# Batch 0 of a fused attention and feed-forward kernel: twelve low planes of the probabilities made by VectorE in place of GpSimd

## The chip, the cores and the metric

The program runs on one core of one Trainium2 chip. A core has TensorE (PE in the profile, PEld for its weight loads), VectorE (DVE), ScalarE (ACT), GpSimd (POOL) and SyncE (SP, which here only issues DMAs). Each engine takes the instructions of its own queue in order, and waits at an instruction until the semaphores of all that it needs are set. The metric is the device time of one execution in microseconds (us).

## The reference

Eight batches, eight heads, 512 local and 32 global positions, head size 64. Local queries see a band of 32 positions to either side and all global keys; global queries see everything. The result goes through a feed-forward layer with the activation h*cos(h).

```python
s_ll = where(|pos_q - pos_k| <= 32, scale * q_l @ k_l.T, -1e9)
s_l  = concat([scale * q_l @ k_g.T, s_ll])        # softmax over both
out_l = softmax(s_l) @ concat([v_g, v_l])
out_g = softmax(scale * q_g @ concat([k_g, k_l]).T) @ concat([v_g, v_l])
x = concat([out_g, out_l])                        # 4352 tokens x 512
h = x @ w_in                                      # 512 -> 2048
out = (h * cos(h)) @ w_out                        # 2048 -> 512
```

All inputs and outputs are float32.

## The kernel before

**Two planes per operand.** A float32 operand of a product is split into a high float16 plane, the rounded value, and a low one, the remainder, and the product is three float16 matmuls (high by high, high by low, low by high). So every operand costs one instruction that writes the high plane and one that writes value minus high.

**Attention.** The heads of a batch go in four pairs, p = 0 to 3, and the 512 queries of a pair in four query tiles, i = 0 to 3. A tile sees a window of 192, 224, 224 or 192 keys. Per pair and tile: `sc_a` computes the scores of both heads (matmul, line 527), `sc_b` adds the mask and takes the row minimum on VectorE (a custom instruction, line 545) into a tile `t` of six rotating buffers, `sc_c` is the exponential on ScalarE with the row sum beside it (line 425), `sc_d` multiplies `t` by the reciprocal row sum (`sm`, lines 564 and 565, on VectorE) and writes the two float16 planes into `planes[i]`, `sc_e` transposes the planes, and `av_a` multiplies them by the values (line 645). In batch 0 the transposition is done on TensorE (line 609), and VectorE (tiles 0 and 2) or ScalarE (tiles 1 and 3) copies the result out of PSUM (line 610). A `t` buffer is free for a later tile as soon as the instruction that computes the low plane has read it.

**Ways to make planes.** `sc_d` takes a code per pair and tile; in batch 0 from the table `PLS`, one row per pair and one entry per tile.

```python
if pl in (3, 4):
    if pl == 3:  # GpSimd scales t, one instruction per head (line 578)
    if pl == 4:  # ScalarE scales t, one instruction per head (line 581)
    nc.scalar.copy(hi, t)                                    # L584, both heads
    for h in range(2):
        nc.gpsimd.tensor_tensor(lo[:, h], t[:, h], hi[:, h], op=ALU.subtract)  # L586
else:
    for h in range(2):
        a = nc.scalar.activation(hi, t[:, h], AF.Identity, scale=r)            # L592
        d = nc.vector.scalar_tensor_tensor(lo, t[:, h], r, hi,
                                           op0=ALU.mult, op1=ALU.subtract)     # L593
```

Pair 3 of batch 0 and all other batches use code 1, the last branch.

**The weights.** `w_in` and `w_out` arrive as float32 in halves or eighths and are split too. For `w_in` the eight pieces k = 0 to 7 are loaded (`w_in_load`, lines 284 and 295), their largest value is taken on VectorE (`w_in_max`, line 246 on `raw_wi`), a scale is derived by a row of very small VectorE instructions (lines 261, 262, 311, 315), and each piece is decoded by ScalarE (line 227) and VectorE (lines 228 and 232) and split by ScalarE (line 239) and GpSimd (line 213). The raw buffers hold four pieces at a time, so a later load waits until GpSimd has read an earlier piece. `w_in_done` turns the largest of all values into the factor `xs` that scales the attention's result (lines 665 and 666), so no product with `w_in` can start before all eight pieces have been looked at. The maxima of `w_out` (line 246 on `wo_hl` and `raw_wm`) are wanted later, for `w_out_done`.

**Order.** From batch 1 on, attention of a later batch is spread between the chunks of the feed-forward part. A chunk is 256 tokens: products `ph` with `w_in` (line 801), activation (lines 823 to 846), products `po` with `w_out` (lines 860 to 862). Ahead of them stands a prologue, in which batch 0's attention and the splitting of `w_in` share VectorE, ScalarE and GpSimd. The code gives each step a slot and a phase, and these become priorities; within them the instructions of each queue are put in order when the program is built, by a planner that keeps a timeline of its own. So a change in one step can also alter the order around it.

Of the kernel before, what the change touches and what calls it, by code (L numbers as in the profile page):

```python
# [62 lines left out]
GFB = 3  # L63
GFW = 3
UW = 1
PLS = [[3, 4, 3, 4], [3, 4, 3, 4], [3, 4, 3, 4], [1, 1, 1, 1]]
TPE = [1, 1, 1, 1]
TPV = [1, 0, 1, 0]
WLV = 0
# [49 lines left out]
def body(tc, qf, v, wi, wo, mask, out):  # L119
# [5 lines left out]
    with ExitStack() as ctx:  # L125
# [441 lines left out]
        def sc_d(b, p, i):  # L567
# [3 lines left out]
            w = WIN[i][1]  # L571
            pl = PLS[p][i] if b == 0 else (PL0, PL1, PL)[min(b, 2)]
            if pl in (3, 4):
# [511 lines left out]
```

## Time and profile before

| | |
|---|---|
| time, median of 3 executions | 959.86 us (959.55 to 961.06) |
| the profiled execution, its own time | 959.23 us |
| its span, first to last instruction | 957.5 us |
| mean granted TensorE clock | 0.965 |
| busy: PE, DVE, ACT, POOL | 909.4, 569.3, 668.4, 399.7 us |

Rows of the profile give the engine, the line of the code, the operation, output and inputs by the program's names, the shapes as partitions x elements, and times. In a timeline row the first number is the start and the second the length, both in us; several instructions of one kind in a row are merged (x4), whatever their shapes, and a bracket says how long the engine had been idle and which instruction released it. In a table of stretches "DVE busy 9.79" is busy time in us within that stretch, and "(x38)" the number of instructions.

### The profile page before, as it was taken

The page shows a single profiled execution, that of the slowest core. Times are in us where ns is not written, and L with a number is a line of the kernel's source. Part 1 is how long each engine was busy: PE and PEld are TensorE (multiplying, and loading weights), DVE is VectorE, ACT ScalarE, POOL GpSimd, SP SyncE. Part 2 cuts the span into 40 slices and gives each one's busy share as a digit, 9 for nine tenths or more (in the row PEclk, how much of TensorE's full clock was granted, in tenths as well). Part 3 has the DMA queues.
Part 4 walks back from the last instruction along what each step waited for, and adds up shares of the span by engine and source line. Part 5 has one row for each costly group of instructions (what it writes and reads, how often), then busy time and mean ns, then how long its engine had stood idle before and what let it go on. Part 6 is the DMA issues. An engine that isn't in the chain of part 4 may idle for free.

```text
span 957.5 us, 20487 instructions
## 1 busy us (share of the span) xinstructions
PE 909.4 (95%) x7963; PEld 604.0 (63%) x7963; DVE 569.3 (59%) x1544; ACT 668.4 (70%) x1435; POOL 399.7 (42%) x412
## 2 busy tenths in 40 slices
PE   6657989999999999999999999999999999999995
PEld 4446656656666666666666666666666666766663
DVE  5987978746565656566655656564746554423231
ACT  7886899957787677766777778777777775443341
POOL 5856654443334243434343333324343434444441
PEclk8667989999999999999999999999999999999998
DMA  9936167745232533545262725342443333000000
GB/s 371 386 121 198 34 163 162 152 111 125 49 108 43 157 63 71 108 122 111 56 122 50 183 46 129 46 146 46 119 61 71 81 68 58 23 1 23 1 24 22
DMA packets 155178, 96.44 MB, mean 101 GB/s; under 512 B 141000, under 2 KB 141128, under 8 KB 153288
## 3 DMA queue, kind: packets, MB, share of 16 engines
q1 hardware_dynamic: 155080, 95.13, 39.6%
q8 instruction: 62, 1.02, 0.4%
q14 instruction: 36, 0.29, 0.1%
HBM read 51.59 MB, written 8.91 MB: 63 GB/s over the span
## 4 chain that ended last, share of the span: by engine, by line
PE 51%; ACT 15%; DVE 11%; issue 9%; POOL 8%; DMA 5%; SPq 0%; ACTq 0%; POOLq 0%; DVEq 0%
PE ph L801 21%; PE po L861 8%; PE po L862 8%; PE po L860 8%; ACT t L425 4%; DMA vr<-v 3%; POOL w L839 3%; PE ps L527 3%; POOL gl L846 2%; ACT planes L592 2%; PE acc L645 2%; DVE gf L841 2%; ACT gh L845 2%; ACT L425 2%; POOL wi_l L213 2%
## 5 line engine op out<-in xcount | busy, mean ns | idle before, releaser
L801 PE MATMUL ph<-xh,wi_h 128*128 128x256 f16 x1024 | 280.7, 274 | 0.9 <-DVE gf L841 0.5
L801 PE MATMUL ph<-xl,wi_h 128*128 128x256 f16 x1024 | 279.8, 273 | 0.0
L801 PE MATMUL ph<-xh,wi_l 128*128 128x256 f16 x1024 | 279.8, 273 | 0.0
L846 POOL TENSOR_TENSOR gl<-gf,gh 128x512 f16<-128x512 f32 x136 | 163.4, 1202 | 237.1 <-ACT gh L845 237.0
L839 POOL TENSOR_TENSOR w<-w 128x512 f32<-128x512 f32 x136 | 143.6, 1056 | 259.1 <-ACT w L425 241.2
L801 PEld LDWEIGHTS <-wi_h 128*128 128x128 f16 x2176 | 205.9, 98 | 55.4 <-issue 18.8
L861 PE MATMUL po<-wo_hl,gh 128*128 128x512 f16 x544 | 206.7, 380 | 0.6 <-POOL wo_hl L213 0.6
L860 PE MATMUL po<-wo_hl,gh 128*128 128x512 f16 x544 | 204.7, 380 | 1.7 <-ACT wo_hl L239 1.7
L862 PE MATMUL po<-wo_hl,gl 128*128 128x512 f16 x544 | 206.3, 380 | 0.0
L845 ACT CAST gh<-gf 128x512 f16<-128x512 f32 x136 | 83.4, 615 | 112.8 <-DVE gf L841 112.7
L824 DVE SCALAR_TENSOR_TENSOR u<-u,cm,ph 128x512 f32<-128x512 f32 x136 | 101.1, 744 | 101.0 <-ACT u L823 101.0
L841 DVE SCALAR_TENSOR_TENSOR gf<-w,ph 128x512 f32<-128x512 f32 x136 | 93.1, 684 | 110.6 <-POOL w L839 110.1
L425 ACT ACTIVATE w<-u,ca 128x512 f32<-128x512 f32 x136 | 98.1, 722 | 84.4 <-DVE u L824 83.5
L425 ACT ACTIVATE t<-t,mn 128x192 f32<-128x192 f32 (+1 forms) x256 | 117.3, 463 | 18.5 <-DVE mn L545 18.1
L801 PEld LDWEIGHTS <-wi_l 128*128 128x128 f16 x1088 | 106.7, 98 | 13.4 <-issue 0.5
L823 ACT ACTIVATE u<-ph,cm 128x512 f32<-128x512 f32 x136 | 92.3, 679 | 25.2 <-PE ph L801 25.2
L593 DVE SCALAR_TENSOR_TENSOR planes<-t,sm,planes 128x192 f16<-128x192 f32 (+1 forms) x232 | 97.8, 481 | 12.0 <-ACT planes L592 11.2
L545 DVE CUSTOM_DVE_ANT_0 t<-ps,msk 128x192 f32<-128x192 f32 (+1 forms) x256 | 83.2, 367 | 18.0 <-PE ps L527 14.8
L862 PEld LDWEIGHTS <-gl 128*128 128x128 f16 x544 | 53.3, 98 | 63.1 <-issue 0.9
L592 ACT ACTIVATE planes<-t,sm 128x192 f16<-128x192 f32 (+1 forms) x232 | 86.3, 458 | 0.0
L861 PEld LDWEIGHTS <-gh 128*128 128x128 f16 x544 | 53.3, 98 | 51.5 <-issue 2.5
L860 PEld LDWEIGHTS <-gh 128*128 128x128 f16 x544 | 52.8, 98 | 51.4 <-issue 2.6
(149 smaller groups left out, 1098.5 us busy)
## 6 DMA issues: line engine op xcount, KB each, us to landing
qkr<-qf SPq DMA_DIRECT2D x31, 608.0 KB, 5.0
vr<-v SPq DMA_DIRECT2D x8, 1280.0 KB, 6.5
out<-o SPq DMA_DIRECT2D x34, 256.0 KB, 2.0
raw_wi<-wi SPq DMA_DIRECT2D x6, 1024.0 KB, 12.2
wo_hl<-wo SPq DMA_DIRECT2D x8, 512.0 KB, 12.7
raw_wm<-wo SPq DMA_DIRECT2D x8, 512.0 KB, 5.7
raw_wo<-wo SPq DMA_DIRECT2D x8, 512.0 KB, 4.4
raw_wi<-wi SPq DMA_DIRECT2D x4, 512.0 KB, 12.3
```

The source lines that it names most:

```text
L425: ins = nc.scalar.activation(*a, **k).ins
L592: a = nc.scalar.activation(hi, t[:, h], AF.Identity, scale=r)
L593: d = nc.vector.scalar_tensor_tensor(lo, t[:, h], r, hi, op0=ALU.mult, op1=ALU.subtract)
L801: nc.tensor.matmul(ph[:, a], w[:, kc, f], x[:, kc, q], start=first and ip == 0, stop=last and ip == 2, skip_group_check=True,)
L824: nc.vector.scalar_tensor_tensor(u, u, m, ph, op0=ALU.subtract, op1=ALU.subtract)
L839: nc.gpsimd.tensor_tensor(w, w, w, op=ALU.mult)
L841: nc.vector.scalar_tensor_tensor(gf, w, 0.5, st.pop(("ph", c, j)).rearrange("p a b -> p (a b)"), op0=ALU.subtract, op1=ALU.mult,)
L845: nc.scalar.copy(gh, gf)
L846: nc.gpsimd.tensor_tensor(gl, gf, gh, op=ALU.subtract)
L860: nc.tensor.matmul(po[k], gh[:, q], wo_h[:, f], start=(f == 0), stop=False)
L861: nc.tensor.matmul(po[k], gh[:, q], wo_l[:, f], start=False, stop=False)
L862: nc.tensor.matmul(po[k], gl[:, q], wo_h[:, f], start=False, stop=(f == NJ - 1))
```

## The change

In the first three pairs of batch 0, tiles 1 and 3 change from code 4 to code 1. Before, ScalarE scaled `t` in place (two instructions), ScalarE copied it into the high plane (one instruction over both heads), and GpSimd subtracted (two instructions). After, ScalarE scales and rounds into the high plane in one step (two instructions), and VectorE multiplies and subtracts in one step (two instructions). Tiles 0 and 2 keep code 3, pair 3 keeps code 1.

```diff
-PLS = [[3, 4, 3, 4], [3, 4, 3, 4], [3, 4, 3, 4], [1, 1, 1, 1]]
+PLS = [[3, 1, 3, 1], [3, 1, 3, 1], [3, 1, 3, 1], [1, 1, 1, 1]]
```

## The prediction

> **What bounds the kernel now.** I read the page first: span, busy times, and the slices.
>
> ```profile
> span 957.5 us, 20487 instructions
> ...
> PE   6657989999999999999999999999999999999995
> ...
> DVE  5987978746565656566655656564746554423231
> ACT  7886899957787677766777778777777775443341
> POOL 5856654443334243434343333324343434444441
> ```
>
> A slice is 23.9 us. From the seventh slice to the last but one TensorE reads 9, so time is won or lost only ahead of that, in the prologue, and there VectorE and ScalarE have the high digits. The changed instructions stand in the first three slices. Next the prologue cut into stretches:
>
> ```profile
> core 0: us, PE busy (x) PEld busy (x) DVE busy (x) ACT busy (x) POOL busy (x), PEclk, DMA share, GB/s
> 24.00:42.00 18.00, 12.78 (x112) 7.80 (x112) 16.54 (x44) 17.02 (x43) 14.17 (x25) 0.54 1.02 414
> 42.00:50.00 8.00, 3.78 (x32) 2.45 (x30) 5.81 (x26) 6.36 (x16) 7.70 (x14) 0.83 1.10 322
> 50.00:54.00 4.00, 1.68 (x14) 1.41 (x14) 3.66 (x7) 4.00 (x10) 2.22 (x2) 0.50 0.95 374
> 54.00:62.30 8.30, 7.42 (x86) 5.66 (x87) 8.20 (x22) 5.88 (x12) 8.23 (x14) 0.58 0.17 70
> 62.30:73.00 10.70, 5.22 (x45) 3.73 (x43) 10.42 (x46) 10.67 (x19) 1.64 (x3) 0.76 0.01 2
> ...
> 84.00:100.00 16.00, 13.51 (x209) 11.03 (x208) 11.69 (x28) 10.55 (x18) 5.69 (x5) 0.89 0.59 195
> 100.00:130.00 30.00, 29.37 (x198) 17.96 (x196) 28.18 (x69) 27.50 (x52) 21.91 (x25) 1.00 0.17 65
> 130.00:200.00 70.00, 65.20 (x556) 40.06 (x555) 55.00 (x165) 68.89 (x164) 28.54 (x32) 0.95 0.69 152
> ```
>
> TensorE is not the bound before 84 us. VectorE is: 8.20 of 8.30 us and then 10.42 of 10.70. ScalarE stands beside it up to 42 us, full up to small gaps. From 100 us TensorE idles only 0.6 and then 4.8 us, so a shift at the end of the prologue reaches the end of the span nearly one to one. Then the timeline, for what makes VectorE idle and who waits for it:
>
> ```profile
> 21.48 0.36 DVE L545 CUSTOM_DVE_ANT_0 t<-ps,msk 128x192 f32<-128x192 f32 x1 [0.21 <-POOL planes L586]
> 32.19 2.40 DVE L232 SCALAR_TENSOR_TENSOR raw_wi<-raw_wi 128x1024 uint32<-128x1024 uint32 x2 [0.79 <-ACT raw_wi L227]
> 37.59 0.39 DVE L545 CUSTOM_DVE_ANT_0 t<-ps,msk 128x224 f32<-128x224 f32 x1 [0.44 <-POOL planes L586]
> 46.62 0.69 DVE L246 TENSOR_REDUCE ws<-raw_wi 128x1 f32<-128x512 f32 x1 [0.42 <-POOL ws L305]
> 49.73 0.39 DVE L545 CUSTOM_DVE_ANT_0 t<-ps,msk 128x224 f32<-128x224 f32 x1 [1.76 <-POOL planes L586]
> 54.10 0.36 DVE L545 CUSTOM_DVE_ANT_0 t<-ps,msk 128x192 f32<-128x192 f32 x1 [0.44 <-POOL planes L586]
> 54.66 1.22 DVE L246 TENSOR_REDUCE ws<-raw_wi 128x1 f32<-128x1024 f32 x1
> 62.33 2.55 ACT L227 ACTIVATE raw_wi<-raw_wi,ws 128x512 f32<-128x512 f32 x3 [2.45 <-DVE ws L262]
> 71.36 12.50 POOL L213 TENSOR_TENSOR wi_l<-raw_wi,wi_h 128x256 f16<-128x256 f32 x16 [9.12 <-ACT wi_h L239]
> ```
>
> The reader is to see two things. Four times VectorE's row minima (L545) wait for a `t` buffer that GpSimd has not yet read, 0.21 + 0.44 + 1.76 + 0.44 = 2.85 us. And from 54.1 us the `w_in` maximum at 54.66 leads, all on VectorE, to the scale for which ScalarE waits 2.45 us (62.33); ScalarE then feeds GpSimd (71.36). So whatever time VectorE has at 54 us is handed on.
>
> **The change part by part.** Durations by shape, between 10 and 80 us:
>
> ```profile
> L586 POOL TENSOR_TENSOR planes<-t,planes 128x192 f16<-128x192 f32 x12 | 8.6, 741 | 5.6 <-ACT planes L584 5.6
> L586 POOL TENSOR_TENSOR planes<-t,planes 128x224 f16<-128x224 f32 x12 | 7.5, 645 | 0.9 <-ACT planes L584 0.9
> L584 ACT CAST planes<-t 128x448 f16<-128x448 f32 x6 | 3.6, 601 | 0.0
> L584 ACT CAST planes<-t 128x384 f16<-128x384 f32 x6 | 3.1, 549 | 0.0
> L581 ACT ACTIVATE t<-t,sm 128x224 f32<-128x224 f32 x6 | 2.6, 504 | 2.7 <-DVE sm L565 2.6
> L581 ACT ACTIVATE t<-t,sm 128x192 f32<-128x192 f32 x6 | 2.5, 474 | 0.0
> L592 ACT ACTIVATE planes<-t,sm 128x224 f16<-128x224 f32 x4 | 1.6, 466 | 0.0
> L592 ACT ACTIVATE planes<-t,sm 128x192 f16<-128x192 f32 x4 | 1.6, 436 | 0.0
> L593 DVE SCALAR_TENSOR_TENSOR planes<-t,sm,planes 128x192 f16<-128x192 f32 x4 | 1.6, 410 | 0.0
> L593 DVE SCALAR_TENSOR_TENSOR planes<-t,sm,planes 128x224 f16<-128x224 f32 x4 | 1.5, 444 | 0.0
> L213 POOL TENSOR_TENSOR wi_l<-raw_wi,wi_h 128x256 f16<-128x256 f32 x26 | 20.1, 805 | 9.1 <-ACT wi_h L239 9.1
> ```
>
> Six tiles change, three of 224 keys and three of 192, two heads each.
>
> GpSimd loses 6 x 0.645 + 6 x 0.741 = 8.3 us. Directly I count this at nothing: GpSimd then idles 9.12 us before 71.36 whatever it did earlier. It counts where somebody waited for it, below. SyncE and GpSimd's queue lose no DMA; a `w_in` load that waits for GpSimd to free a raw buffer may start earlier, but the maximum at 54.66 follows on VectorE without any wait for a DMA, so I count zero; if VectorE came earlier than the data, that load would be the next wait.
>
> ScalarE loses 6 x 0.504 + 6 x 0.474 of scaling and 3 x 0.601 + 3 x 0.549 of rounding, and gains 6 x 0.466 + 6 x 0.436: 9.3 out, 5.4 in, 3.9 us less. After 54 us it waits for VectorE anyway (2.45 us), so this too counts only through VectorE's waits, the 0.79 us at 32.19.
>
> VectorE gains 6 x 0.444 + 6 x 0.410 = 5.1 us, 1.7 us per pair, in the stretches up to 62.30 where pairs 0 to 2 are worked on, on the engine that binds. The rows of these durations lie in a time without GpSimd work (62.30 to 73.00, 1.64 us busy). Behind each low plane stand the next row minima and the weight work in VectorE's queue; its own wait is for ScalarE's high plane. The transposes on TensorE wait for the low plane, and TensorE has room.
>
> What VectorE gets back: of tiles 1 and 3 it now frees the `t` buffer itself, and GpSimd does half the work for the others. I take all four waits, 2.85 us, plus 0.42 at 46.62 (a tiny GpSimd instruction queued behind other GpSimd work) and 0.79 at 32.19: 4.1 us. The lower end is 0 (the waits return, on GpSimd for tiles 0 and 2 or on ScalarE's high plane), the upper end is 4.1, and I take the upper because of what ends the one large wait:
>
> ```profile
> 48.50 1.19 POOL L586 TENSOR_TENSOR planes<-t,planes 128x224 f16<-128x224 f32 x2
> ```
>
> These two end at 49.69, just before VectorE starts at 49.73. Two 224-wide subtractions taken alone, before any 192-wide one of the pair, are those of tile 1, which is a changed tile: its `t` is then free right after VectorE's own low plane.
>
> Last, not all of VectorE's work before 62 us is urgent. The maxima of `w_out` are wanted only after the last one:
>
> ```profile
> 87.99 0.69 DVE L246 TENSOR_REDUCE wos<-raw_wm 128x1 f32<-128x512 f32 x1 [3.47 <-DMA raw_wm<-wo]
> ```
>
> VectorE waits 3.47 us there, and idles 4.31 us between 84 and 100. Each such maximum that slips back there takes its 0.69 us off the urgent stretch. I take one, 0.7 us; ends 0 and two, 1.4.
>
> Sum: 5.1 - 4.1 - 0.7 = +0.3 us. The profiled execution took 959.23 us, which becomes 959.5; the median of the three is 0.63 us above it, so on that footing 960.2 us. This is within 0.2% (1.9 us), which is about what a measurement of this kernel can tell from no change.
>
> **A rule about who blocks whom.** Row first: the 192-wide GpSimd subtraction took 741 ns on the mean, the 224-wide one 645, although it has fewer elements. Some of the 192-wide ones ran beside VectorE's joins of two inputs, until 53.67:
>
> ```profile
> 50.96 2.71 DVE L232 SCALAR_TENSOR_TENSOR raw_wi<-raw_wi 128x1024 uint32<-128x1024 uint32 x2
> ```
>  The Trainium skill, page "SBUF — State Buffer", section "SBUF: two separate sides", says why that can be: GpSimd and VectorE share one pair of ports under an exclusive lock, and a VectorE operation with two SBUF inputs takes part in it, the later one waiting for the whole of the earlier. By that rule the twelve new low planes, each with two inputs, can be held up by GpSimd; the page gives no price for this case. From rows:
>
> ```profile
> L593 DVE SCALAR_TENSOR_TENSOR planes<-t,sm,planes 128x192 f16<-128x192 f32 (+1 forms) x232 | 97.8, 481 | 12.0 <-ACT planes L592 11.2
> ```
>
> Over the whole run, with GpSimd working beside it, the low plane took 481 ns on the mean against 427 for the eight quiet ones: 12 x 0.054 = 0.6 us more. The other end: GpSimd is busy 24.1 of the 30 us from 24 to 54, and half of its 805 ns piece at each meeting makes 12 x 0.8 x 0.4 = 3.9 us. I take neither into the forecast, since twelve GpSimd subtractions that could hold up VectorE go at the same time; it is a rival.
>
> **The rivals.**
>
> *Faster: the chain through GpSimd and ScalarE is what matters.* For it, the chain of waits between 10 and 62 us by line:
>
> ```profile
> by line: POOL planes L586 11.3%; ACT t L425 11.2%; POOL wi_l L213 10.7%; ACT raw_wi L227 8.6%; ACT t L581 8.2%; ACT planes L584 7.6%; ACT vh L476 6.9%; DVE raw_wi L228 5.3%; DVE wos L246 4.6%; DVE pt L610 4.5%; issue 4.5%; DVE ws L246 4.3%;
> ```
>
> Of 52 us L586 has 5.9 and L584 4.0. Half of both goes, 4.9 us. If half of the new low planes, 2.6 us, come onto the chain in their place, 2.3 us are won: 957.6 us. At the most, with all lows hidden, 4.9: 955.0. Against it: VectorE's idle time from 24 to 62.30 is only 4.1 us in all.
>
> *Slower: VectorE's own work.* The low planes stand ahead of the weight work in VectorE's queue and only the waits of the third pair, 1.76 + 0.44, come back, as the others are followed by queues that ScalarE fills: 5.1 - 2.2 = +2.9, 962.8 us. With nothing back, 965.0. It decides against "no change" once less than 3.2 of the 5.1 us come back. For it: after 54.1 us VectorE hardly idles. Against it: the movable `w_out` maxima.
>
> *Slower: the lock.* The 3.9 us above on top of +0.3: 964.1 us. Against it, the measured mean of 481 ns.
>
> *The order changes.* Queues are planned anew, so pieces may change places as far as 200 us; TensorE's idle 4.8 us between 130 and 200 could go or double. This has either sign, I count it in the width of all cases and not as one of its own.
>
> **How the numbers follow.** Forecast, no change to speak of: 0.35. Chain rival: 0.33. VectorE rival: 0.24, lock: 0.08. So faster by over 0.2% 0.33, within 0.35, slower 0.32. The predicted time is 960.2 us. The likeliest case's own range is 958.3 to 961.8. The range over all cases runs from 956.0, which leaves out the last part of the chain rival, to 965.0, VectorE with nothing back; I leave some 2 in 10 outside.
>
> **What would show it.** Right: 24 - 12 = 12 subtractions on GpSimd's L586, 6 on L584, none on L581, 20 low planes on L593 before 80 us at 410 to 480 ns; VectorE's waits for POOL planes down from 2.85 us to under 0.5; the scale for ScalarE at 62.33 within 1 us of where it was, and so the long GpSimd run at 71.36. The chain rival shows both of these earlier by 2 us or more; the VectorE rival later by 2 or more with VectorE busy throughout; the lock in L593 far above 481 ns on the mean before 60 us. What makes the forecast wrong is mostly its second term, the 4.1 us: if the waits turn up again behind ScalarE's high planes, or if removing them lets the whole chain move.

## The result: 0.95% slower, and the profile after

The changed kernel takes 968.29 us (median of 5, 967.79 to 970.5), the kernel before beside it 959.55 us (median of 5). The ratio is 1.0095, 95% interval 1.0079 to 1.011: 9.1 us slower. The forecast was 960.2 us, range 956.0 to 965.0, so the time lies outside it. Below, a difference in us is always (ratio - 1) x 959.6 us.

The head of the page and four of its slice rows, of the changed kernel:

```profile
span 966.0 us, 20485 instructions
...
PE 911.7 (94%) x7963; PEld 607.9 (63%) x7963; DVE 577.7 (60%) x1556; ACT 665.8 (69%) x1429; POOL 393.3 (41%) x400
...
PE   6657988899999999999999999999999999999996
...
DVE  5998978846575666556565656564756555323231
ACT  6895799866777677776777778767777766434341
POOL 4745744423434343433333343424343434344441
```

TensorE reads 9 throughout from the ninth slice on, before from the seventh: slices seven and eight, 145 to 193 us, now read 8. They lie long after the changed steps. The table of stretches of the changed kernel, same stretches as before:

```profile
core 0: us, PE busy (x) PEld busy (x) DVE busy (x) ACT busy (x) POOL busy (x), PEclk, DMA share, GB/s
24.00:42.00 18.00, 12.74 (x100) 8.46 (x97) 16.62 (x48) 17.82 (x39) 12.83 (x21) 1.00 1.09 388
42.00:50.00 8.00, 5.11 (x51) 3.87 (x49) 8.00 (x23) 5.23 (x15) 7.66 (x12) 0.76 0.60 174
50.00:54.00 4.00, 3.05 (x24) 2.42 (x25) 4.00 (x11) 2.33 (x5) 3.44 (x6) 0.50 0.92 349
54.00:62.30 8.30, 6.40 (x69) 5.31 (x68) 8.30 (x24) 8.25 (x22) 0.10 (x1) 0.50 0.73 305
62.30:73.00 10.70, 3.12 (x20) 1.63 (x19) 10.66 (x34) 10.40 (x16) 6.09 (x9) 0.66 0.01 2
84.00:100.00 16.00, 13.23 (x197) 10.88 (x196) 13.14 (x34) 9.41 (x17) 6.16 (x8) 0.82 0.70 217
100.00:130.00 30.00, 29.43 (x204) 18.53 (x203) 26.23 (x59) 24.68 (x51) 21.17 (x24) 0.99 0.19 66
130.00:200.00 70.00, 59.54 (x493) 37.38 (x492) 54.75 (x154) 65.05 (x148) 30.18 (x34) 0.95 0.68 150
```

Two things differ. From 42 to 62.30 us VectorE has no gap left: 8.00, 4.00 and 8.30 us, where it was 5.81, 3.66 and 8.20. And from 130 to 200 us TensorE idles 10.5 us instead of 4.8, while ScalarE, which had idled 2.5 + 1.1 us from 100 to 200, idles 5.3 + 5.0. No instruction there was changed. Two rows of the waits of the changed kernel between 80 and 205 us name the partners (us in total, times, longest):

```profile
ACT w L425 <- DVE u L824: 7.5, 5, 3.4
PE po L860 <- ACT wo_hl L239: 7.0, 5, 2.9
```

and the same two waits of the kernel before:

```profile
ACT w L425 <- DVE u L824: 2.0, 2, 1.2
PE po L860 <- ACT wo_hl L239: 1.7, 2, 1.1
```

ScalarE's longest wait of the first kind, in the timelines of VectorE, GpSimd and ScalarE of the changed kernel:

```profile
111.50 3.57 DVE L512 SCALAR_TENSOR_TENSOR vl<-vr,vs,vh 128x640 f16<-128x640 f32 x2
114.99 0.73 DVE L824 SCALAR_TENSOR_TENSOR u<-u,cm,ph 128x512 f32<-128x512 f32 x1
111.52 2.87 POOL L846 TENSOR_TENSOR gl<-gf,gh 128x512 f16<-128x512 f32 x2
115.76 0.72 ACT L425 ACTIVATE w<-u,ca 128x512 f32<-128x512 f32 x1 [3.40 <-DVE u L824]
```

ScalarE stands still for 3.40 us because the fifth L824 (two of the expectations call it the sixth) stands in VectorE's queue behind four low planes of batch 1's values (L512), the last two stretched to 3.57 us beside GpSimd. In the kernel before, the fifth L824 started at 103.58 us and the sixth at 109.25, both ahead of the first L512 at 110.56. So the planner put the queues in another order here, far from the change. (ScalarE has one longer wait, 6.55 us for VectorE's L410 at 89.74 us; below, a run that wins most of the time back has it too.)

Now the changed planes of the changed kernel, groups between 10 and 80 us:

```profile
L593 DVE SCALAR_TENSOR_TENSOR planes<-t,sm,planes 128x224 f16<-128x224 f32 x10 | 6.3, 676 | 1.5 <-ACT planes L592 1.4
L593 DVE SCALAR_TENSOR_TENSOR planes<-t,sm,planes 128x192 f16<-128x192 f32 x10 | 6.3, 648 | 0.0
L586 POOL TENSOR_TENSOR planes<-t,planes 128x224 f16<-128x224 f32 x6 | 4.9, 833 | 0.0
L586 POOL TENSOR_TENSOR planes<-t,planes 128x192 f16<-128x192 f32 x6 | 4.1, 710 | 1.1 <-ACT planes L584 1.1
```

Counts are as forecast, 20 and 12, but a low plane takes 676 and 648 ns, not 444 and 410. And four rows of its timelines, one from the middle and three from the end of the urgent stretch:

```profile
32.62 1.31 DVE L593 SCALAR_TENSOR_TENSOR planes<-t,sm,planes 128x224 f16<-128x224 f32 x2 [1.38 <-ACT planes L592]
64.02 0.68 DVE L246 TENSOR_REDUCE wos<-raw_wm 128x1 f32<-128x512 f32 x1
64.81 0.14 DVE L262 TENSOR_SCALAR ws<-ws 128x1 uint32<-128x1 uint32 x1
72.50 6.71 POOL L213 TENSOR_TENSOR wi_l<-raw_wi,wi_h 128x256 f16<-128x256 f32 x8 [3.05 <-ACT wi_h L239]
```

### The profile page after: what moved, and what is told of

The parts are those of the page before. It is cut to its first block, busy times and chain, and to the rows that moved or that the text cites. A ratio compares the mean times of both kernels' runs of the same rounds, so it can differ in the third digit from the quotient of the medians.

```text
span 966.0 us, 20485 instructions
## 1 busy us (share of the span) xinstructions
PE 911.7 (94%) x7963; PEld 607.9 (63%) x7963; DVE 577.7 (60%) x1556; ACT 665.8 (69%) x1429; POOL 393.3 (41%) x400
## 4 chain that ended last, share of the span: by engine, by line
PE 60%; ACT 6%; issue 5%; POOL 4%; DVE 3%; DMA 2%; ACTq 0%; POOLq 0%
PE ph L801 26%; PE po L860 9%; PE po L861 9%; PE po L862 9%; PE ps L527 3%; PE acc L645 3%; DMA vr<-v 2%; POOL w L839 2%; POOL gl L846 2%; ACT t L425 2%; ACT planes L592 1%; ACT gh L845 1%; DVE gf L841 1%; PE gps L682 1%; PE gacc L737 1%
## 5 line engine op out<-in xcount | busy, mean ns | idle before, releaser
L846 POOL TENSOR_TENSOR gl<-gf,gh 128x512 f16<-128x512 f32 x136 | 161.9, 1192 | 241.2 <-ACT gh L845 241.2
L824 DVE SCALAR_TENSOR_TENSOR u<-u,cm,ph 128x512 f32<-128x512 f32 x136 | 101.1, 744 | 103.3 <-ACT u L823 103.3
L841 DVE SCALAR_TENSOR_TENSOR gf<-w,ph 128x512 f32<-128x512 f32 x136 | 93.2, 685 | 116.2 <-POOL w L839 115.7
L593 DVE SCALAR_TENSOR_TENSOR planes<-t,sm,planes 128x224 f16<-128x224 f32 (+1 forms) x244 | 111.0, 513 | 13.6 <-ACT planes L592 12.7
L592 ACT ACTIVATE planes<-t,sm 128x224 f16<-128x224 f32 (+1 forms) x244 | 90.9, 457 | 0.7 <-DVE sm L565 0.5
```

The source lines that it names most:

```text
L593: d = nc.vector.scalar_tensor_tensor(lo, t[:, h], r, hi, op0=ALU.mult, op1=ALU.subtract)
L824: nc.vector.scalar_tensor_tensor(u, u, m, ph, op0=ALU.subtract, op1=ALU.subtract)
L841: nc.vector.scalar_tensor_tensor(gf, w, 0.5, st.pop(("ph", c, j)).rearrange("p a b -> p (a b)"), op0=ALU.subtract, op1=ALU.mult,)
L846: nc.gpsimd.tensor_tensor(gl, gf, gh, op=ALU.subtract)
```

## The experiments

Two theories stood after this: the **work** theory (VectorE's added and stretched planes are handed on) and the **order** theory (the queues planned anew cost it). To separate them, a kernel plans its program twice, first with the other table, and then ties each queue to the order found there. The ties are order alone, between neighbours in one queue that both plans have, without a wait across engines; steps that only one plan has stay free.

```diff
+        mine = {k: i for i, k in keys.values()}
+        for names in kept or ():              # one list per queue in KEPT, of the steps in SLOTS
+            last = None
+            for k in names:
+                if k in mine:
+                    if last is not None:
+                        tc.add_manual_dep(mine[k], last.name, order, reason="kept_order")
+                    last = mine[k]
...
+        body(tc, **targs, codes=DONOR, keys=seen)     # the plan of the other table, on a twin program
```

In the first four runs these lines shift the kernel's own lines by 5 (L593 is L598). The code excerpts below write the tables short. What the ties themselves cost is seen in two runs further down that keep nearly all of the old work in the old order: ratios 0.9994 and 0.9995, so nothing that can be measured.

### Work and order apart

**The change in the old order.** All five queues are kept.

```diff
 PLS = [[3, 1, 3, 1]] * 3 + [[1, 1, 1, 1]]
+DONOR = [[3, 4, 3, 4]] * 3 + [[1, 1, 1, 1]]
```

> The changed kernel's instructions in the queue order of the kernel before: each instruction that both have keeps its place on its engine, ScalarE's high planes take the places of the scalings, the twelve new low planes go where the planner puts them between the others. The theory that the new order costs the 8.7 us expects 959 to 961 us, so nothing or 1 us over the kernel before. The theory that VectorE's 5.1 us of new low planes cost it expects 965 to 969 us. The forecast's own sum expects +0.3 us.

961.6 us, ratio 1.0023 [1.0013, 1.0032]: +2.2 us. That is 0.6 us over the range of the order theory and far under that of the work theory. So in the old order the work costs 2.2 us, and the new order adds 6.9 to reach 9.1.

**The old work in the new order.**

```diff
 PLS = [[3, 4, 3, 4]] * 3 + [[1, 1, 1, 1]]
+DONOR = [[3, 1, 3, 1]] * 3 + [[1, 1, 1, 1]]
```

> The kernel before's instructions (scalings and roundings on ScalarE, subtractions on GpSimd) in the queue order of the changed kernel. The theory of the order expects 966 to 970 us, as slow as the changed kernel. The theory of VectorE's work expects 958 to 962 us. If each has half, about 964.

972.9 us, ratio 1.0142 [1.0125, 1.0159]: +13.6 us, more than either theory had. The old work alone becomes slow in the new order, by more than the changed kernel is. So the order costs time without the change's work, and the two do not simply add: in the old order the change's work costs 2.2 us, in the new order it is 4.5 us faster than the old work (9.1 against 13.6).

### Where the order costs its time

**Old order in the prologue alone, and from slot 0 on alone,** all five queues.

```diff
+SLOTS = (None, 0)     # e3: prologue
+SLOTS = (0, None)     # e4: all later slots
```

> The change with the old order kept among the steps of the prologue alone (slots below 0); the steps from the first chunk on are planned anew. If the loss comes of the prologue's new order, 960 to 962 us; if it comes of the order of the steps after it (batch 1's attention, the splitting of w_out, the first chunks), 965 to 969; by the theory of VectorE's work also 965 to 969.

> The change with the prologue planned anew and the old order kept among the steps from slot 0 on. If the loss comes of the order after the prologue, 960 to 963 us (some 1 to 3 us of the prologue's delay may stay); if it comes of the prologue's order or of VectorE's work, 965 to 969.

971.0 us, 1.0118 [1.0102, 1.0135], and 962.93 us, 1.0025 [1.0012, 1.0039]. With the old order from slot 0 on, the prologue, where the change is, may be planned anew at no cost (2.4 us against 2.2); the order from slot 0 on is the expensive one. The first of the two is slower than its 965 to 969 us: its later steps got one more new plan, not that of the changed kernel.

**By queue, from slot 0 on:** TensorE alone; all but TensorE; ScalarE alone.

```diff
+KEPT = ['PE']                                   # e5
+KEPT = ['Activation', 'DVE', 'Pool', 'SP']      # e6
+KEPT = ['Activation']                           # e7
```

> The change, planned anew, but among the steps from slot 0 on TensorE alone keeps the old order. Theory P: the loss of the order lies in TensorE's queue, which stands at products with w_out (po) whose pieces ScalarE has not split yet (7.0 us of such waits against 1.7 before): then 962 to 964 us. Theory S: it lies in the order of ScalarE's and VectorE's queues, which lets ScalarE idle at 111.6 to 115.8 us and finish the pieces late: then 966 to 970 us.

> The change, planned anew, but from slot 0 on ScalarE, VectorE, GpSimd and SyncE keep the old order and TensorE alone has a new one. Theory P: 966 to 970 us. Theory S: 962 to 964 us.

> The change, planned anew, with only ScalarE's old order kept from slot 0 on. If ScalarE's own queue order is the cause, 962 to 964 us; if VectorE's place for the activation's second step (L824), behind four low planes of the values, is what makes ScalarE wait, or TensorE's order, 966 to 970 us.

964.44 us, 1.0048 [1.0033, 1.0063]; 962.67 us, 1.0034 [1.0021, 1.0047]; 969.75 us, 1.0103 [1.0086, 1.012]. TensorE's order gives 4.5 of the 9.1 us back, all the others' 5.9, ScalarE's alone nothing. So neither theory has it: each side alone goes a good part of the way. Of the last kernel's five executions the profiled one took 962.98 us, the others 969.49 to 970.89, so its trace does not show its median. The same program can go either way there; that is not explained.

**By stretch, and VectorE alone.** All five queues in slots 0 to 15 (to about 205 us), all five in slots 16 on, and VectorE's queue alone from slot 0 on.

```diff
+SLOTS = (0, 16)                        # e13
+SLOTS = (16, None)                     # e14
+KEPT = ['DVE']; SLOTS = (0, None)      # e15
```

> The change, with the old order of the queues kept only for the steps of slots 0 to 15, which the trace of before shows to end near 205 us; prologue and all later slots are planned anew. Theory (the cost lies where batch 1's attention and w_out's pieces stand between the first two chunks, where ScalarE's idle time from 100 to 200 us went from 3.6 to 10.3 us): as with the old order in all slots from 0 on, 962.9 us, 962 to 964, and ScalarE idle 5 to 7 us. Rival (the new order costs a little in every chunk): half way, 965 to 966.5. Rival (what counts is where the two plans meet): as slow as the changed kernel, 968.

> The change, with the old order kept only for the steps from slot 16 on (after about 205 us). Theory: the loss has been made by then, 967 to 970 us. Rival (cost in every chunk): 964 to 966. Together with the run before it, the two should add up to the 5.4 us that the old order from slot 0 on gave back, if the stretches do not act on each other.

> The change, with the old order kept for slots from 0 on VectorE's queue only. Theory (VectorE's activation step L824 stands behind two long low planes of the values, L512, and ScalarE waits for it): VectorE's order alone gives most of it back, 962.5 to 964.5 us, and the waits of ScalarE's L425 for VectorE's u fall from 7.5 us to under 3. Rival (no single queue but TensorE's, as ScalarE's alone gave nothing): 967 to 970.

962.71 us, 1.0025 [1.0016, 1.0034]; 970.38 us, 1.0102 [1.0088, 1.0116]; 960.78 us, 1.0008 [1.0, 1.0017]. The whole cost of the order is made in the first 16 slots, and tying VectorE's queue alone takes it away, more fully than its 962.5 to 964.5 us expected. That does not make VectorE's queue the only one that matters, as the planner places the other queues around the tied one. Take the longest series of instructions, matched by line, tiles and shape, that two traces have in the same order between 85 and 205 us. Of ScalarE's 236 in the kernel before, the changed kernel has 121 in that order, and the one with VectorE tied 209; of TensorE's 975 matmuls they have 697 and 837. So the tie brings most of the old order back on these engines too. The stretches from 130 to 200 us, of slots 0 to 15 kept, of slots 16 on kept, and of VectorE kept:

```profile
130.00:200.00 70.00, 64.10 (x556) 40.10 (x555) 57.05 (x171) 68.81 (x160) 31.48 (x35) 0.98 0.67 150
```

```profile
130.00:200.00 70.00, 59.41 (x495) 37.52 (x494) 54.89 (x155) 65.08 (x147) 30.65 (x35) 0.95 0.68 150
```

```profile
130.00:200.00 70.00, 66.31 (x559) 41.75 (x557) 55.57 (x168) 68.26 (x159) 30.64 (x35) 0.93 0.65 150
```

The second is the changed kernel's row again (59.54 and 65.05); in the other two ScalarE is back at 68 to 69 us and TensorE at 64 to 66. (The profiled execution with VectorE kept took 962.93 us, the slowest of its eleven; the granted clock in its row is 0.93 against 0.95 to 0.98 in the others, so TensorE's busy time is not quite like for like.) The run of slots 0 to 15 has the 6.7 us wait for L410 too, so that wait is not what costs. With VectorE kept, the wait that had grown to 7.5 us is gone:

```profile
ACT w L425 <- DVE u L824: 0.2, 1, 0.2
```

**Which of VectorE's steps.** Old order on VectorE in slots 0 to 15 between L512, L824 and L841 only; and of all its steps, in slots 0 to 7 (to about 140 us).

```diff
+KEPT = ['DVE']; SLOTS = (0, 16); steps v_d, m1_b, m1_d only      # e17
+KEPT = ['DVE']; SLOTS = (0, 8)                                   # e18
```

> The change, with the old order kept on VectorE's queue alone, in slots 0 to 15, and there only between the values' low planes (L512) and the activation's two steps (L824, L841); all other steps find their places anew around them. Theory (the four L512 planes ahead of the sixth L824, with ScalarE waiting 3.4 us for it, start the loss): most of the 7 us that VectorE's whole old order gave back, 961 to 964 us, and ScalarE's waits for VectorE's u under 3 us in place of 7.5. Rival (the loss is made by the mix of w_out's pieces and batch 1's planes too): 965 to 970 us, with ScalarE idle over 8 us from 100 to 200 us.

> The change, with the old order kept on VectorE's queue alone and there only for the steps of slots 0 to 7, up to about 140 us. Theory (the loss begins at the sixth L824, near 115 us, and what follows in the second chunk only inherits it): as with VectorE's whole old order, 960.8 us, 960 to 963. Rival (the second chunk, where batch 1's planes stand between the w_out pieces, loses by itself): 964 to 969 us, with batch 1's last pair (L665) still beyond 200 us.

966.17 us, 1.0058 [1.0039, 1.0076], and 966.28 us, 1.0058 [1.0037, 1.008]. Each gives back 3.6 of the 9.1 us, where VectorE's whole order gave 8.3. By the times, the rival has it in both runs: the swap of the values' low planes is part of the loss and not all of it, and so is the order of VectorE's steps after slot 7. The first run also shows its rival's mark, ScalarE idle for 8.8 us from 100 to 200 us, and its waits for VectorE's `u` fell to 3.4 us. For the last run its rival's mark is not there: the last pair of batch 1 (L665) stands at 196 us, not beyond 200. From 130 to 200 us its ScalarE is back at 68.1 us, but TensorE only at 62.1. TensorE's matmuls wait there most for another partner, 2.6 us in all in the kernel before and 2.3 with VectorE's whole order kept:

```profile
PE acc L645 <- DMA pt<-planes: 5.4, 5, 2.5
```

Which further steps of VectorE's queue cost the rest stays open.

### Does the order follow the size of the change?

A rival was that any edit draws an order at random, good or bad. Pair 2 alone in the old order, and pairs 0, 1, 2 each alone and planned anew:

```diff
+PLS[2] = [3, 1, 3, 1]; DONOR = the table of before      # e8
+PLS[0] (e10), PLS[1] (e11) or PLS[2] (e12) = [3, 1, 3, 1], no DONOR
```

> Only pair 2's tiles 1 and 3 changed, everything in the old order. This is where VectorE waited 1.76 and 0.44 us for GpSimd. Theory of work less waits: four low planes at 0.57 us are 2.3 us, waits of 2.6 us come back: 959 to 960 us, not slower. Theory that every low plane costs its full time: 961 to 962 us.

> Only pair 0's two tiles changed, planned anew. Its work alone is 4 low planes of 0.7 us, some 2 us. Theory that a new plan is a draw with an error of its own of several us: the three kernels of this kind (pair 0, 1 or 2 alone) scatter by 5 us or more, in no relation to their work, one perhaps under the kernel before. Theory that the plan gets worse in step with the change: each 1 to 4 us over the kernel before, 961 to 964.

> Only pair 1's two tiles changed, planned anew. As for pair 0: a scatter of 5 us or more among the three by the theory of the draw, 961 to 964 us by the theory of steady worsening.

> Only pair 2's two tiles changed, planned anew. In the old order this change took 959.3 us, 0.9994 of the kernel before. Theory of the draw: anything from 955 to 970 us. Theory of steady worsening: 959 to 962.

Old order, pair 2: 959.32 us, 0.9994 [0.9984, 1.0003]. Planned anew: 964.17 us, 1.0051 [1.0035, 1.0066]; 964.48 us, 1.005 [1.0031, 1.007]; 963.19 us, 1.0039 [1.0026, 1.0052]. Each third of the change costs 3.7 to 4.9 us when planned anew, and pair 2's work nothing that can be measured when it is not. Pairs 0 and 1 lie just over the 961 to 964 us of steady worsening, pair 2 over its 959 to 962. The three add to 13.4 us against 9.1 for all, so the cost does not grow in step with the change, and three draws that all fall within 1.2 us of each other do not look like chance with a wide scatter. So neither theory holds as it was put. That every new plan seen here is slower than the old one fits an old order that stands well above what the planner usually finds; four plans do not prove it.

### Whether GpSimd's reading stretches VectorE's planes

The first run's kernel, with GpSimd's work of the prologue on probabilities, values and `w_in` replaced by writing zeros: same places in the queue, no operand read. It leaves those low planes, and the scaling of tiles 0 and 2, out.

```diff
-nc.gpsimd.tensor_tensor(lo[:, h], t[:, h], hi[:, h], op=ALU.subtract)      # also L578, L509, L213 of w_in
+nc.gpsimd.memset(lo[:, h], 0.0)
```

> The change in the old order, with GpSimd's scalings and subtractions of the prologue (probabilities, values of batch 0, low plane of w_in) replaced by writes of zeros to the same places, so that GpSimd reads nothing there; these planes are thus zero. Theory of the shared port: the new low planes all take 400 to 450 ns (in e1 those beside GpSimd took 670 to 740), and 1.5 us or more is won, 957 to 960 us. Theory that they are slow for another reason (place, PSUM, waiting for ScalarE): some still take 600 ns or more.

955.97 us, 0.9967 [0.9952, 0.9982]: 5.4 us less than with GpSimd reading, and below the 957 to 960 us expected. Here is VectorE's low plane before 80 us, all 20 instructions, as minimum/median/maximum in ns, of the changed kernel, of the change in the old order, and with GpSimd reading nothing:

```profile
L593 DVE SCALAR_TENSOR_TENSOR planes<-t,sm,planes x20: 405/702/866, 15.7 to 70.7; 128x224 f16<-128x224 f32 x10, 128x192 f16<-128x192 f32 x10
```

```profile
L598 DVE SCALAR_TENSOR_TENSOR planes<-t,sm,planes x20: 404/443/742, 16.5 to 72.6; 128x224 f16<-128x224 f32 x10, 128x192 f16<-128x192 f32 x10
```

```profile
L593 DVE SCALAR_TENSOR_TENSOR planes<-t,sm,planes x20: 406/428/452, 16.7 to 69.8; 128x224 f16<-128x224 f32 x10, 128x192 f16<-128x192 f32 x10
```

Without GpSimd's reads no plane is longer than 452 ns. The traces with GpSimd's reads say the same plane by plane: in the changed kernel the 16 planes that ran beside a GpSimd instruction took 535 to 866 ns, the four others 405 to 441; in the old order the six that ran beside one throughout took 673 to 742, all others 404 to 445. So the stretching comes from GpSimd's work beside it. That it is the reading, and not that GpSimd is merely busy less, rests on the only two planes which ran beside its zeros, in the timelines of VectorE and GpSimd:

```profile
47.20 0.81 DVE L593 SCALAR_TENSOR_TENSOR planes<-t,sm,planes 128x224 f16<-128x224 f32 x2
46.96 1.05 POOL L240 MEMSET wi_l<- 128x256 f16 x4
```

Two of 224 columns in 0.81 us is the quiet duration (447 and 445 ns). The 5.4 us are not the price of the stretching alone, as writing zeros also takes GpSimd less time (328 and 253 ns in place of 718 and 612).

### A version that might beat both

VectorE was almost full from 62.30 to 73.00 us (10.42 of 10.70) and GpSimd there at 1.64, so tiles 0 and 2 of pair 3 were given to GpSimd, in the kernel before and its order.

```diff
 PLS[0:3] = [3, 4, 3, 4]
-PLS[3] = [1, 1, 1, 1]
+PLS[3] = [3, 1, 3, 1]
+DONOR = the table of before
```

> The kernel before, in its own order, with pair 3's tiles 0 and 2 by GpSimd (code 3) in place of ScalarE and VectorE: VectorE loses four low planes of 0.410 to 0.444 us, 1.7 us, in the stretch from 54 to 73 us, where it was busy 18.6 of 19.0 us and GpSimd 9.9. Theory (VectorE binds there and hands its shift on one to one): 1.0 to 1.7 us faster than before, 957.9 to 958.6 us. Rival (GpSimd's planes come later than VectorE's would, and the transposes of pair 3 wait for them; its two scalings and two subtractions of 0.65 to 0.74 us a tile are a chain of some 3 us): no change or up to 2 us slower, 959.6 to 961.6 us.

959.71 us, 0.9995 [0.9986, 1.0003]: no change, as the rival had it, and not the 957.9 to 958.6 us of the theory. VectorE in that stretch, and how it had begun:

```profile
14.26 0.16 DVE L479 TENSOR_REDUCE vm<-vm 128x1 f32<-128x4 f32 x1 [1.94 <-ACT vh L476]
63.44 0.14 DVE L262 TENSOR_SCALAR ws<-ws 128x1 uint32<-128x1 uint32 x1
68.59 2.06 DVE L593 SCALAR_TENSOR_TENSOR planes<-t,sm,planes 128x224 f16<-128x224 f32 x4
73.04 0.34 DVE L366 TENSOR_SCALAR xs<-xs,gam 128x4 f32<-128x4 f32 x1
```

This execution is 1.3 us late at 14 us already (12.94 before) and still at the scale (62.16 before). At `xs` it is 0.6 us late (72.43 before), so 0.7 us of the 1.7 were won in between; the four planes left to VectorE took 0.52 us each, as two of them now stand beside GpSimd (739 and 707 ns). At the end nothing of it can be measured, though the interval, -1.3 to +0.3 us, would still hold the 0.7. No version here that computes all of the result beats the kernel before.

## Why the prediction was wrong, point by point

**What bounds it, and handing on one to one: right in the old order only.** The change in the old order, on VectorE:

```profile
14.15 0.16 DVE L484 TENSOR_REDUCE vm<-vm 128x1 f32<-128x4 f32 x1 [1.96 <-ACT vh L481]
65.14 0.14 DVE L267 TENSOR_SCALAR ws<-ws 128x1 uint32<-128x1 uint32 x1
```

The scale is 3.0 us later than before (62.16), 1.2 us of which this execution has at 14 us already (12.94 before), ahead of any changed step; the span is 2.3 us longer (959.8). In the changed kernel the scale is 2.7 us later (64.81) and the long GpSimd run 1.1 (72.50): "within 1 us" was missed, and the marks of the slower VectorE rival, a scale later by 2 us or more and VectorE full, came up; so did that of the lock, low planes far above 481 ns. But the newly planned prologue does not hand its delay on. The factor `xs`, and TensorE's first product with the low plane of x, before and in the changed kernel:

```profile
72.43 0.26 DVE L366 TENSOR_SCALAR xs<-xs,gam 128x4 f32<-128x4 f32 x1
80.94 0.42 PE L801 MATMUL ph<-xl,wi_h 128*128 128x256 f16 x1
```

```profile
77.14 0.36 DVE L366 TENSOR_SCALAR xs<-xs,gam 128x4 f32<-128x4 f32 x1
82.87 0.37 PE L801 MATMUL ph<-xl,wi_h 128*128 128x256 f16 x1 [1.20 <-DVE xl L666]
```

`xs` is 4.7 us later and the product 1.9. With VectorE's later order kept `xs` is as late (77.98), and the time is 0.8 us over the kernel before. Where the rest of that delay is absorbed was not followed.

**Failed step: the order.** "This has either sign, I count it in the width of all cases and not as one of its own." It is the largest term, +6.9 us on top of the work's 2.2, and the range did not hold it. The place was named rightly, TensorE's idle 4.8 us between 130 and 200 us "could go or double"; it became 10.5. It went without a price though the kernel is planned anew for every edit. Its price could not be read from the trace of before; a case of its own for "slower by a few us" belonged there, as the old order is the one that the time before was read from.

**Failed step: the size of the low planes.** 5.1 us for twelve, at durations from a stretch without GpSimd work. Old order: the two groups of the change in the old order,

```profile
L598 DVE SCALAR_TENSOR_TENSOR planes<-t,sm,planes 128x192 f16<-128x192 f32 x10 | 5.1, 522 | 0.0
L598 DVE SCALAR_TENSOR_TENSOR planes<-t,sm,planes 128x224 f16<-128x224 f32 x10 | 4.5, 501 | 0.1
```

make 9.6 us of busy time, less the 3.1 of pair 3 before: 6.5. In the changed kernel 6.3 + 6.3 - 3.1 = 9.5 us. The forecast counted mean times number; by that measure, which counts twice where the end of one plane and the start of the next overlap, the term is 6.8 and 9.8 us, so 1.7 and 4.7 over the forecast. In the old order six of the twelve new planes stood beside GpSimd for their whole length. In the changed kernel all twelve met it and cost 3.0 us more, inside the rival's 0.6 to 3.9; the other 1.7 us lie on four planes of pair 3, which GpSimd's `w_in` pieces now stand beside. "I take neither into the forecast" was the mistake: the row of 481 ns over the whole run spoke for the lower bound, but is a mean over meetings and quiet times. The Trainium skill, page "SBUF — State Buffer", section "SBUF: two separate sides", says that a VectorE operation with two SBUF inputs and a GpSimd operation that reads SBUF hold each other up; the trace agrees, 702 ns at the median in the changed kernel, where 16 of 20 planes stand beside GpSimd, and 428 ns when GpSimd reads nothing.

**The recovered waits: right in kind, 3.4 of 4.1 us in size.** In the old order the four waits for GpSimd's planes (2.85 us) and the 0.42 us are gone, as read from the one row at 48.50; the 0.79 us for ScalarE at 32.19 became 0.65. In the changed kernel a wait of 1.38 us for ScalarE's high plane appeared at 32.62, the other way that the text named.

**The movable maximum: not got.** 0.7 us. No `w_out` maximum moved back; in the changed kernel one (64.02 above) still stands right in front of the steps to the scale at 64.81.

**GpSimd's 8.3 and ScalarE's 3.9 us freed, counted at nothing: not tested by itself.** The sum below lies 0.9 us over the run in the old order, so a gain of that size is not excluded; the counts of instructions came out as said.

**The sum.** With the measured sizes in busy time the work is 6.5 - 3.4 = +3.1 us; the run in the old order gives +2.2 (1.2 to 3.1). With only VectorE's later order kept, the changed kernel is at 1.0008 [1.0, 1.0017], near the forecast's "no change to speak of"; since two terms were mis-sized, that nearness is luck. Of the rivals, the slower VectorE one and the lock had the mechanism for the work; none had the 6.9 us.

## What to carry to other kernels

Where a planner orders the queues, an edit of one table entry is two changes: keep the old order by force once, and the old work in the new order once, before explaining a time by the instructions. Give the new order a case and a chance of its own in a forecast, above all where the order before was good. Take the duration of a VectorE operation with two inputs from rows where GpSimd runs beside it, if that is where it will stand.

## What was not expected of the hardware

A two-input VectorE plane of 192 or 224 columns takes 404 to 452 ns alone and up to 866 ns beside a reading GpSimd instruction, twice as long; GpSimd writing constants beside it does not show in the two planes that met it (447 and 445 ns). The values' low planes, L512, show the same in the queue: two of them took 3.57 us beside L846 at 111.50 us.
